# Second pass, layer one: shared sums of block products kept in PSUM, seeded by a ScalarE copy

## The chip, the cores and the metric

One Trainium2 chip, one core. The metric is the device time of one execution of the kernel in microseconds (us). Engines: PE (TensorE matrix products), DVE (VectorE), ACT (ScalarE), POOL (GpSimd) and SP, whose queue issues most transfers. PSUM is the memory that PE writes its sums to, in banks; SBUF is the large on-chip memory.

## The reference

Attention with a sigmoid in place of the softmax feeds a gated network (two weights, a squared relu, a sigmoid gate); its output `x` goes through this last part, in which the change lies:

```python
def _moe2_ref(x, w_ch1, w_ch2) -> np.ndarray:
    X = np.fft.fft(x, axis=1)
    X = np.fft.fft(X, axis=2)
    mixed = np.real(X).astype(np.float32)
    u = x + mixed
    mu = np.mean(u, axis=-1, keepdims=True)
    var = np.mean((u - mu) ** 2, axis=-1, keepdims=True)
    un = (u - mu) / np.sqrt(var + 1e-06)
    ch = np.maximum(un @ w_ch1, 0.0) @ w_ch2
    return (u + ch).astype(np.float32)
```

The batch is 4, the sequence 448, the model width 768; `w_ch1` is 768 x 3072 and `w_ch2` 3072 x 768. All is float32.

## The kernel before, in words

Every large product is made of float32 values split in a high and a low part of 12 bits, with three matmuls (high x high, high x low, low x high) into one PSUM bank of 128 x 448 sums. The last network (`w_ch1` is layer one, `w_ch2` layer two) runs in two passes. The first takes batches 0 and 1 directly. The second pass, which takes batches 2 and 3 together, is where the change lies; it needs fewer products, by Winograd's form of Strassen's scheme: a 2 x 2 block product out of seven block products of sums and differences of the blocks, whose results share partial sums.

Layer one of the second pass is `pair1(g, _)`, called for the twelve groups g = 0 to 11 of 256 hidden columns. Each call takes the seven entries of the table `PRODUCTS` in order; in this document they are n = 0 to 6. An entry names the weight block (A11, S2, ...), the rows block (B11, T2, ...) and the bank (X, Y, Z or W) that its nine matmuls of 448 columns add to. After each product `after(n)` reads its bank:

- n = 0 (A11 B11): ACT copies X to SBUF, `u2`.
- n = 1 (S2 T2): DVE adds bank Y to `u2`.
- n = 2 (S3 T3): DVE makes `u3` = `u2` + Z.
- n = 3 (S1 T1): DVE adds W to `u3`, which is the result block c22 and goes through the relu in `result`.
- n = 4 (A12 B21): added on X by PE; the result is read from the bank.
- n = 5 (A22 T4): added on Z by PE; DVE makes `c21` = `u2` + Z.
- n = 6 (S4 B22): added on W by PE; DVE adds W to `u2`.

PE may add to a bank only when it has been read: `step` starts n = 4 after the ACT copy, n = 5 after `u3`, n = 6 after the c22 add (the `need` of `c1`, `u3`, `c22`).

What else runs at that time. The pass goes `pair1` of groups 0 and 1, and then, five times, `second` (layer two, products k = 0 to 4), `pair1` of an even group, `second` (k = 5 and 6), `pair1` of an odd group. `second_weights` makes the layer-one blocks (`blk`) out of raw weights `a` that SP loads from DRAM, `second_weights2` the layer-two blocks (`sw`) out of raw weights `w` (tiles `w2_1` to `w2_4`, four transfers each), `second_rows` the layer-two rows (`hs`) out of the tile `rows`. All of them cast on ACT and subtract on DVE. `second_done` copies each finished layer-two bank to one of six `stage` slots on ACT and POOL then adds it into DRAM by a transfer (`u_d<-stage`).

The order of the work on each engine is fixed before the launch: the class `Order` keeps a clock with estimated costs (lines 200 to 262 of the profile are its helpers: L200 every matmul, L235 a DVE add or subtract, L252 an ACT copy or cast, L254 an ACT activation, L261 a transfer), and each helper issues its instruction when its inputs should be there by that clock. On the chip each engine takes its instructions in that order, and waits for what an instruction needs even if a later one could run. Banks come from `bank` (two, and a third for every third call) and `bank2` (five).

Of the kernel before, what the change touches and what calls it, by code (L numbers as in the profile page):

```python
# [16 lines left out]
ALU = mybir.AluOpType  # L17
# [3 lines left out]
B, H, S, DH = 4, 12, 448, 64  # L21
# [47 lines left out]
def _dft_tables():  # L69
# [36 lines left out]

PRODUCTS = (
    ("A11", "B11", "X"),
    ("S2", "T2", "Y"),
    ("S3", "T3", "Z"),  # L110
    ("S1", "T1", "W"),
    ("A12", "B21", "X"),
    ("A22", "T4", "Z"),
    ("S4", "B22", "W"),
)
LATE = ("T1", "B21", "T4", "B22")


SECOND = (("A11", "B11"), ("S1", "T1"), ("A12", "B21"), ("S4", "B22"), ("S2", "T2"), ("S3", "T3"), ("A22", "T4"))
# [148 lines left out]
def build(tc, ap):  # L268
    nc = tc.nc
    V, G = nc.vector, nc.gpsimd  # L270
    o = Order(nc)
# [72 lines left out]
    w_d = {nm: [dram.tile([128, D], F32, name=f"{nm}_d{i}") for i in range(2 * NG)] for nm in ("w1", "w2")}  # L344
    t_d = {(nm, d): dram.tile([128, 2, S], F32, name=f"t_d{nm}{d}") for nm in LATE for d in range(3)}
    rs_d = [dram.tile([1, S], F32, name=f"rs_d{b}") for b in range(B)]
# [7 lines left out]
    def bank(name):  # L354
        banked[0] += 1
        if ps1c and banked[0] % 3 == 0:
            return ps1c[0].tile([128, 512], F32, tag="bankc", name=name)
        return ps1.tile([128, 512], F32, tag="bank", name=name)
# [248 lines left out]
    for f in range(NF + KD):  # L607
        if f < NF:
            src, hl, key = ap["w_k"][f], [w[:, f].rearrange(flat) for w in (wkh, wkl)], ("wk", f)
        elif f < NF + HELD:  # L610
            src, hl, key = ap["w_r"][f - NF], [w.rearrange(flat) for w in wr_t[f - NF]], ("wr", f - NF)
# [42 lines left out]
    def bank2(name):  # L654
        return ps1b.tile([128, 512], F32, tag="bank2", name=name)
# [133 lines left out]
    for i, n in enumerate((113, 112, 112, 111)):  # L789
        c = fp.tile([128, 2, TW], F32R, name=f"ct{i}")  # L790
# [335 lines left out]
    def parts_of(out, src, key, eng):  # L1126

        yield o.act(out[0], src)
        o.at[key] = t = o.sub(eng, out[1], src, out[0])
        yield t  # L1130
# [49 lines left out]
    blk_t = {}  # L1180

    def second_weights():

        for g in range(NG):
            w = []
            for j in range(2):
                if g > 0:
                    yield from o.need(("blk", 7 * g - 1))
                t = ws2.tile([128, D], F32, tag=f"w{j}", name=f"a_{g}_{j}", bufs=1)
                at = o.dma(t, w_d["w1"][2 * g + j])  # L1190
                w.append((t, min(at, o.now + 9.0) if g == 1 else at))
            yield max(t for _, t in w)
            (wa, wb), n = (t for t, _ in w), D // 2
            a11, a12, a21, a22 = wa[:, 0:n], wa[:, n:D], wb[:, 0:n], wb[:, n:D]
            s1 = ws2.tile([128, n], F32, tag="s1", name=f"s1_{g}", bufs=1)
            src = {"A11": a11, "S2": a11, "S3": a21, "S1": s1, "A12": a12, "A22": a22, "S4": a12}
            for k, (nm, _, _) in enumerate(PRODUCTS):
                m = 7 * g + k
                if m < 8:
                    yield from o.need(("w1", "used", NG - 2 + m // 4))  # L1200
                else:
                    yield from o.need(("prod", m - 8))
                pl = pools_of["w1"][m % 8 // 4]
                blk_t[m] = pl.tile([128, D], F32R, tag="w1" + "hl"[m % 2], name=f"blk_{m}", bufs=2)
                if nm == "S2":
                    yield o.tt(V, s1, a21, a22, ALU.add)
                    yield o.tt(V, a21, a11, a21, ALU.subtract)
                    yield o.tt(V, a11, s1, a11, ALU.subtract)
                elif nm == "S4":
                    yield o.tt(V, a12, a12, a11, ALU.subtract)  # L1210
                yield from parts_of((blk_t[m][:, 0:n], blk_t[m][:, n:D]), src[nm], ("blk", m), V)
# [42 lines left out]
    def second_rows():  # L1254

        yield from o.need(*(("t_d", nm, 2) for nm in LATE))
        ms = np_.tile([128, 3, 2, S], F32, tag="x2", name="rows", bufs=3)
# [85 lines left out]
    def prepare_rows():  # L1343
# [8 lines left out]
        def put(nm, d, src):  # L1352
            if nm not in LATE:
                t = t_t[nm, d] = tp.tile([128, 2, S], F32R, name=f"{nm}_{d}")
                yield from parts_of((t[:, 0], t[:, 1]), src, ("t", nm, d), V)
                return
            t = np_.tile([128, 2, S], F32R, tag="sq", name=f"{nm}_{d}", bufs=1)
            yield from parts_of((t[:, 0], t[:, 1]), src, ("row", nm, d), V)
            o.at["t_d", nm, d] = t = o.dma(t_d[nm, d], t.bitcast(F32))
            yield t + 2.0  # L1360
# [19 lines left out]
    def late_rows():  # L1380
        for n, (nm, d) in enumerate((nm, d) for nm in LATE for d in range(3)):
            yield from o.need(("w1", "last", n // KD), ("t_d", nm, d))
            t = t_t[nm, d] = kp.tile([128, 2, S], F32R, tag="k2v", name=f"{nm}_{d}", bufs=NK)
            o.at["t", nm, d] = o.dma(t.bitcast(F32), t_d[nm, d])
            yield o.now + 0.2


    def result(g, b, i, src):
        yield from (master if g < 2 * NS else hidden)(g, b, i, src)
# [21 lines left out]
    def network():  # L1411
# [31 lines left out]
        def pair1(g, _):  # L1443

            ps, t = {}, {}

            def tmp(nm):
                tag = {"u2": "sum_u", "u3": "sum_v", "c21": "rsb"}[nm]
                t[nm] = np_.tile([128, S], F32, tag=tag, name=f"{nm}_{g}", bufs=1)
                return t[nm]  # L1450

            def after(n):
                x, y, z, w = (ps[k][:, 0:S] if k in ps else None for k in "XYZW")
                if n == 0:
                    o.at["c1", g] = o.act(tmp("u2"), x)
                elif n == 1:
                    yield from o.need(("c1", g))
                    o.at["u2", g] = o.tt(V, t["u2"], t["u2"], y, ALU.add)
                elif n == 2:
                    yield from o.need(("u2", g))  # L1460
                    o.at["u3", g] = o.tt(V, tmp("u3"), t["u2"], z, ALU.add)
                elif n == 3:
                    yield from o.need(("u3", g))
                    o.at["c22", g] = o.tt(V, t["u3"], t["u3"], w, ALU.add)
                    yield o.at["c22", g]
                    yield from result(g, 3, 1, t["u3"])
                elif n == 4:
                    yield from result(g, 2, 0, x)
                elif n == 5:
                    o.at["c21", g] = o.tt(V, tmp("c21"), t["u2"], z, ALU.add)  # L1470
                    yield o.at["c21", g]
                    yield from result(g, 2, 1, t["c21"])
                else:
                    yield o.tt(V, t["u2"], t["u2"], w, ALU.add)
                    yield from result(g, 3, 0, t["u2"])
                yield o.now

            def step(n, i, lhs, rhs, k):
                if i == 0 and n < 4:
                    ps[k] = (bank2 if k == "Y" else bank)(f"f1_{g}_{k}")  # L1480
                o.mm(ps[k][:, 0:S], lhs, rhs, i == 0 and n < 4, i == 8, skip=True)
                if i == 8:
                    o.at["prod", 7 * g + n] = o.now
                    o.spawn(after(n), o.now + 0.1)

            for n, (_, rows, k) in enumerate(PRODUCTS):
                blk = blk_t.get(7 * g + n)
                yield from o.need(("blk", 7 * g + n))
                yield from o.need(*((key, g) for key in {4: ["c1"], 5: ["u3"], 6: ["c22"]}.get(n, [])))
                blk = blk_t[7 * g + n]  # L1490
                for d in range(3):
                    yield from o.need(("t", rows, d))
                    ws = [blk[:, c : c + 128] for c in (128 * d, D // 2 + 128 * d)]
                    rs = [t_t[rows, d][:, c] for c in range(2)]
                    for i, (a, c) in enumerate(((0, 0), (0, 1), (1, 0))):
                        o.feed.append(partial(step, n, 3 * d + i, ws[a], rs[c], k))
                while len(o.feed) > 6:
                    yield o.now + 0.1
# [39 lines left out]
        for p in range(NS):  # L1538
            order += [(second, "s2", (p, range(5))), (pair1, "p1", (2 * p + 2, 3))]
            order += [(second, "s2", (p, (5, 6))), (pair1, "p1", (2 * p + 3, 3))]  # L1540
# [43 lines left out]
    o.spawn(second_rows())  # L1584
    o.spawn(combine())
    o.spawn(second_weights())
    o.spawn(second_weights2())
    o.run()
# [64 lines left out]
```

## Time and profile before

| | us |
|---|---|
| runs: median of 3 (lowest, highest) | 1159.89 (1159.8, 1160.81) |
| the profiled execution's own time | 1160.56 |
| its span, first to last instruction | 1158.8 |
| PE busy in the span | 1149.8 |
| DVE busy | 792.5 |
| ACT busy | 570.8 |
| layer one and two of the second pass | 848 to 1126 of the span |

The span is one profiled execution; the runs are others, without a profile. In the trace's rows a start is in us from the first instruction. In a timeline row the square bracket is the idle time ahead of the instruction and what ended it. A matmul row lasts longer than it holds the engine, because matmuls overlap; nine matmuls of 448 columns take 1.80 us in the chain of waits, which is what they add to the time. The view of the chain starts a product 0.16 us later than the timeline does.

### The profile page before, as it was taken

How to read it: one execution, taken by the hardware profiler on the slowest of the kernel's cores; microseconds unless marked ns; L12 is line 12 of the kernel's file. 1: busy time of each engine (PE TensorE's matmuls, PEld its weight loads, DVE VectorE, ACT ScalarE, POOL GpSimd, SP SyncE). 2: the span in 40 equal slices, each digit the busy share in tenths (PEclk: the TensorE clock that was granted, in tenths of full speed). 3: DMA queues.
4: the chain of work that ended last, by engine and by line, in shares of the span. 5: the costliest groups of instructions: out<-in, count | busy, mean ns of one | idle time of the engine just before them, and what ended most of it. 6: DMA issues, size and time to landing. Idle time of an engine off the chain costs nothing.

```text
span 1158.8 us, 16593 instructions
## 1 busy us (share of the span) xinstructions
PE 1149.8 (99%) x6094; PEld 1009.0 (87%) x6094; DVE 792.5 (68%) x1333; ACT 570.8 (49%) x1051; POOL 106.7 (9%) x154
## 2 busy tenths in 40 slices
PE   8999999999999999999999999999999999999998
PEld 3476676799999999999999999999999999999998
DVE  3876757576514679898777767775477787777662
ACT  6887887667520133243333333332137567665740
POOL 0000001000000000000000000000003243342420
PEclk9999999999999999999999999999999999999999
DMA  7765789668939355477575657563917696878894
GB/s 234 238 230 201 255 325 336 237 230 285 335 136 290 121 191 199 138 287 273 201 252 195 227 190 236 186 228 123 339 44 176 128 201 109 186 137 170 177 195 167
DMA packets 92550, 243.53 MB, mean 210 GB/s; under 512 B 10610, under 2 KB 46516, under 8 KB 92340
## 3 DMA queue, kind: packets, MB, share of 16 engines
q1 hardware_dynamic: 74596, 204.70, 50.8%
q0 software_dynamic: 17584, 37.30, 17.1%
q8 instruction: 48, 0.79, 0.3%
q10 hardware_dynamic: 288, 0.46, 0.1%
q14 instruction: 34, 0.28, 0.1%
HBM read 145.45 MB, written 99.04 MB: 211 GB/s over the span
## 4 chain that ended last, share of the span: by engine, by line
PE 96%; DMA 1%; ACT 1%; DVE 0%; issue 0%; SPq 0%; DVEq 0%
PE f L200 32%; PE m L200 10%; PE v L200 10%; PE k L200 9%; PE r L200 7%; PE av L200 6%; PE sc L200 5%; PE f_W L200 4%; PE f_X L200 3%; PE f_Z L200 3%; PE f_Y L200 2%; PE pq L200 1%; DMA w<-w_d 1%; PE sc_c L200 1%; PE pa L200 1%; PE qa L200 1%
## 5 line engine op out<-in xcount | busy, mean ns | idle before, releaser
L200 PE MATMUL f<-un,w1h 128*128 128x448 f32 x576 | 164.2, 364 | 0.0
L200 PE MATMUL f<-h,w2h 128*128 128x448 f32 x576 | 163.2, 363 | 0.0
L235 DVE TENSOR_TENSOR acc<-acc,f 128x448 f32<-128x448 f32 x126 | 77.6, 619 | 70.9 <-PE f L200 69.4
L259 POOL DMA_DIRECT2D u_d<-stage x75 | 64.7, 933 | 604.1 <-ACT stage L252 597.1
L200 PEld LDWEIGHTS f<-un,w1h 128*128 128x128 f32 x576 | 108.1, 188 | 7.6 <-issue 0.6
L200 PEld LDWEIGHTS f<-h,w2h 128*128 128x128 f32 x576 | 108.1, 188 | 7.1
L200 PE MATMUL v<-k,wvh 128*128 128x448 f32 x384 | 111.9, 365 | 0.0
L200 PE MATMUL f<-un,w1l 128*128 128x448 f32 x288 | 103.9, 361 | 0.0
L200 PE MATMUL f<-h,w2l 128*128 128x448 f32 x288 | 103.7, 360 | 0.0
L200 PE MATMUL m<-hs,sw_h 128*128 128x448 f32 x324 | 91.5, 363 | 0.0
L254 ACT ACTIVATE sg<-sc,bias_s 128x448 f32<-128x448 f32 x144 | 78.6, 651 | 13.2 <-PE sc L200 13.2
L200 PEld LDWEIGHTS v<-k,wvh 128*128 128x128 f32 x384 | 72.0, 188 | 4.9 <-issue 0.6
L200 PE MATMUL k<-xkh,wkh 128*128 128x448 f32 x192 | 70.6, 368 | 0.9 <-ACT kt L254 0.9
L200 PE MATMUL k<-xkl,wkh 128*128 128x448 f32 x192 | 70.2, 366 | 0.0
L200 PE MATMUL k<-xkh,wkl 128*128 128x448 f32 x192 | 70.1, 365 | 0.0
L200 PE MATMUL v<-k,wvl 128*128 128x448 f32 x192 | 69.7, 363 | 0.0
L254 ACT ACTIVATE h<-f 128x448 fp32r<-128x448 f32 x48 | 26.2, 546 | 81.1 <-PE f L200 81.1
L200 PEld LDWEIGHTS m<-hs,sw_h 128*128 128x128 f32 x324 | 60.8, 188 | 4.0
L252 ACT COPY stage<-m 128x448 f32<-128x448 f32 x105 | 55.7, 535 | 16.0 <-DMA u_d<-stage 9.4
L200 PE MATMUL m<-hs,sw_l 128*128 128x448 f32 x162 | 58.3, 360 | 0.0
L200 PEld LDWEIGHTS f<-un,w1l 128*128 128x128 f32 x288 | 53.9, 187 | 3.9 <-issue 0.2
L200 PE MATMUL av<-sg,v 128*64 128x448 f32 x288 | 57.2, 544 | 0.0
(227 smaller groups left out, 2490.2 us busy)
## 6 DMA issues: line engine op xcount, KB each, us to landing
w_raw<-in_w SPq DMA_DIRECT2D x40, 768.0 KB, 4.9
u_d<-stage POOLq DMA_DIRECT2D x75, 224.0 KB, 6.1
w_d<-w_bits SPq DMA_DIRECT2D x40, 384.0 KB, 2.6
k_d<-kp SPq DMA_DIRECT2D x32, 448.0 KB, 3.9
k<-k_d SPq DMA_DIRECT2D x32, 448.0 KB, 5.6
a<-w_d SPq DMA_DIRECT2D x24, 384.0 KB, 5.5
w<-w_d SPq DMA_DIRECT2D x24, 384.0 KB, 10.4
v<-in_v SPq DMA_DIRECT2D x24, 256.0 KB, 3.5
```

The costliest lines, as they stand in the source:

```text
L200: self.nc.tensor.matmul(out, lhs, rhs, start=start, stop=stop, skip_group_check=skip)
L235: eng.tensor_tensor(out, a, c, op=op)
L252: self.nc.scalar.copy(out, a)
L254: self.nc.scalar.activation(out, a, fn, **kw)
L259: self.nc.gpsimd.dma_start(out, src, accum_op=ALU.add)
```

## The change

The three partial sums are no longer made on DVE but in PSUM, by PE's own addition. The order of the products changes and Z is gone:

- n = 0 (A11 B11) in X; ACT copies bank X into bank Y (the seed).
- n = 1 (S3 T3) in W; ACT copies W to SBUF, `w7`.
- n = 2 (S2 T2) is added on the seed in Y; ACT copies Y to SBUF, `u2`.
- n = 3 (A12 B21) is added on X; the result is read from the bank.
- n = 4 (S1 T1) is added on Y; DVE adds Y to `w7`, which is c22.
- n = 5 (A22 T4) is added on W; DVE adds W to `u2`, which is c21.
- n = 6 (S4 B22) is added on Y; the result is read from the bank.

PE now starts n = 2 after the seed, n = 4 after the copy `u2`, n = 5 after the copy `w7`, n = 6 after the c22 add. X and W come from `bank2`, Y from `bank`. The rows blocks that are loaded late are loaded in the new order of use (B21 ahead of T1).

```diff
@@ -106,14 +106,14 @@
 
 PRODUCTS = (
     ("A11", "B11", "X"),
+    ("S3", "T3", "W"),
     ("S2", "T2", "Y"),
-    ("S3", "T3", "Z"),
-    ("S1", "T1", "W"),
     ("A12", "B21", "X"),
-    ("A22", "T4", "Z"),
-    ("S4", "B22", "W"),
+    ("S1", "T1", "Y"),
+    ("A22", "T4", "W"),
+    ("S4", "B22", "Y"),
 )
-LATE = ("T1", "B21", "T4", "B22")
+LATE = ("B21", "T1", "T4", "B22")
 
 
 SECOND = (("A11", "B11"), ("S1", "T1"), ("A12", "B21"), ("S4", "B22"), ("S2", "T2"), ("S3", "T3"), ("A22", "T4"))
@@ -1202,7 +1202,7 @@
                     yield from o.need(("prod", m - 8))
                 pl = pools_of["w1"][m % 8 // 4]
                 blk_t[m] = pl.tile([128, D], F32R, tag="w1" + "hl"[m % 2], name=f"blk_{m}", bufs=2)
-                if nm == "S2":
+                if nm == "S3":
                     yield o.tt(V, s1, a21, a22, ALU.add)
                     yield o.tt(V, a21, a11, a21, ALU.subtract)
                     yield o.tt(V, a11, s1, a11, ALU.subtract)
@@ -1445,48 +1445,43 @@
             ps, t = {}, {}
 
             def tmp(nm):
-                tag = {"u2": "sum_u", "u3": "sum_v", "c21": "rsb"}[nm]
+                tag = {"u2": "sum_u", "w7": "sum_v", "c": "rsb"}[nm]
                 t[nm] = np_.tile([128, S], F32, tag=tag, name=f"{nm}_{g}", bufs=1)
                 return t[nm]
 
             def after(n):
-                x, y, z, w = (ps[k][:, 0:S] if k in ps else None for k in "XYZW")
+                x, y, w = (ps[k][:, 0:S] if k in ps else None for k in "XYW")
                 if n == 0:
-                    o.at["c1", g] = o.act(tmp("u2"), x)
+                    ps["Y"] = bank(f"f1_{g}_Y")
+                    o.at["seed", g] = o.act(ps["Y"][:, 0:S], x)
                 elif n == 1:
-                    yield from o.need(("c1", g))
-                    o.at["u2", g] = o.tt(V, t["u2"], t["u2"], y, ALU.add)
+                    o.at["w7", g] = o.act(tmp("w7"), w)
                 elif n == 2:
-                    yield from o.need(("u2", g))
-                    o.at["u3", g] = o.tt(V, tmp("u3"), t["u2"], z, ALU.add)
+                    o.at["u2", g] = o.act(tmp("u2"), y)
                 elif n == 3:
-                    yield from o.need(("u3", g))
-                    o.at["c22", g] = o.tt(V, t["u3"], t["u3"], w, ALU.add)
+                    yield from result(g, 2, 0, x)
+                elif n == 4:
+                    o.at["c22", g] = o.tt(V, t["w7"], t["w7"], y, ALU.add)
                     yield o.at["c22", g]
-                    yield from result(g, 3, 1, t["u3"])
-                elif n == 4:
-                    yield from result(g, 2, 0, x)
+                    yield from result(g, 3, 1, t["w7"])
                 elif n == 5:
-                    o.at["c21", g] = o.tt(V, tmp("c21"), t["u2"], z, ALU.add)
-                    yield o.at["c21", g]
-                    yield from result(g, 2, 1, t["c21"])
+                    yield o.tt(V, t["u2"], t["u2"], w, ALU.add)
+                    yield from result(g, 2, 1, t["u2"])
                 else:
-                    yield o.tt(V, t["u2"], t["u2"], w, ALU.add)
-                    yield from result(g, 3, 0, t["u2"])
+                    yield from result(g, 3, 0, y)
                 yield o.now
 
             def step(n, i, lhs, rhs, k):
-                if i == 0 and n < 4:
-                    ps[k] = (bank2 if k == "Y" else bank)(f"f1_{g}_{k}")
-                o.mm(ps[k][:, 0:S], lhs, rhs, i == 0 and n < 4, i == 8, skip=True)
+                if i == 0 and n < 2:
+                    ps[k] = bank2(f"f1_{g}_{k}")
+                o.mm(ps[k][:, 0:S], lhs, rhs, i == 0 and n < 2, i == 8, skip=True)
                 if i == 8:
                     o.at["prod", 7 * g + n] = o.now
                     o.spawn(after(n), o.now + 0.1)
 
             for n, (_, rows, k) in enumerate(PRODUCTS):
-                blk = blk_t.get(7 * g + n)
                 yield from o.need(("blk", 7 * g + n))
-                yield from o.need(*((key, g) for key in {4: ["c1"], 5: ["u3"], 6: ["c22"]}.get(n, [])))
+                yield from o.need(*((key, g) for key in {2: ["seed"], 3: ["seed"], 4: ["u2"], 5: ["w7"], 6: ["c22"]}.get(n, [])))
                 blk = blk_t[7 * g + n]
                 for d in range(3):
                     yield from o.need(("t", rows, d))
```

Where the instructions stand. The first place is DVE in group 6, around the add that n = 6 of PE waits for. Names: `sw_3` is the sum of raw layer-two weights made from `w2_3`; `u3_6` + `f1_6_W` is c22 before. Before:

```order
L235 TENSOR_TENSOR sw_21_l_9814<-w2_3_9729,sw_21_h_9813 128x768
L235 TENSOR_TENSOR u3_6_9825<-u2_6_9791,f1_6_Z_9804 128x448
L235 TENSOR_TENSOR blk_48_9808<-a_6_0_9567,blk_48_9808 128x384
L235 TENSOR_TENSOR sw_3_9812<-w2_3_9729 128x768
L235 TENSOR_TENSOR u3_6_9825<-u3_6_9825,f1_6_W_9823 128x448
L235 TENSOR_TENSOR w2_3_9729<-w2_3_9729 128x2x384
L235 TENSOR_TENSOR w2_3_9729<-sw_3_9812,w2_3_9729 128x2x384
L235 TENSOR_TENSOR c21_6_9865<-u2_6_9791,f1_6_Z_9804 128x448
```

And now, where `w7_6` + `f1_6_Y` is c22:

```order
L235 TENSOR_TENSOR blk_48_9776<-a_6_0_9541,blk_48_9776 128x384
L235 TENSOR_TENSOR sw_21_l_9802<-w2_3_9713,sw_21_h_9801 128x768
L235 TENSOR_TENSOR sw_3_9800<-w2_3_9713 128x768
L235 TENSOR_TENSOR w2_3_9713<-w2_3_9713 128x2x384
L235 TENSOR_TENSOR w2_3_9713<-sw_3_9800,w2_3_9713 128x2x384
L235 TENSOR_TENSOR w7_6_9791<-w7_6_9791,f1_6_Y_9778 128x448
L235 TENSOR_TENSOR u2_6_9811<-u2_6_9811,f1_6_W_9774 128x448
```

The c22 add stood behind one instruction on the raw weights `w2_3`, and stands behind three now; in group 8 it is the same.

The second place is DVE in group 2, before (c22 is the second row with `u3_2`):

```order
L235 TENSOR_TENSOR u3_2_8865<-u2_2_8837,f1_2_Z_8852 128x448
L235 TENSOR_TENSOR sw_7_l_8871<-w2_1_8780,sw_7_h_8870 128x768
L235 TENSOR_TENSOR u3_2_8865<-u3_2_8865,f1_2_W_8863 128x448
L235 TENSOR_TENSOR sw_1_8869<-w2_1_8780 128x768
L235 TENSOR_TENSOR w2_1_8780<-w2_1_8780 128x2x384
L235 TENSOR_TENSOR w2_1_8780<-sw_1_8869,w2_1_8780 128x2x384
L235 TENSOR_TENSOR c21_2_8905<-u2_2_8837,f1_2_Z_8852 128x448
```

And now (c22 is `w7_2`):

```order
L235 TENSOR_TENSOR sw_7_l_8847<-w2_1_8764,sw_7_h_8846 128x768
L235 TENSOR_TENSOR sw_1_8845<-w2_1_8764 128x768
L235 TENSOR_TENSOR w2_1_8764<-w2_1_8764 128x2x384
L235 TENSOR_TENSOR w2_1_8764<-sw_1_8845,w2_1_8764 128x2x384
L235 TENSOR_TENSOR w7_2_8851<-w7_2_8851,f1_2_Y_8832 128x448
```

Here the c22 add stood ahead of the three, and stands behind them now. In group 4 it stood behind the first of them and now stands behind the first two.

The third place is ACT in group 10, at the copy of bank X. Now (before, the same rows stand ahead of the copy `u2_10<-f1_10_X`, though in a slightly other order):

```order
L252 CAST hs_34_1_10696<-rows_8109 128x448
L252 COPY stage_8315<-m_32_1_10681 128x448
L252 CAST blk_75_10705<-a_10_1_10490 128x384
L252 COPY stage_8315<-m_32_2_10693 128x448
L252 COPY f1_10_Y_10728<-f1_10_X_10709 128x448
L252 CAST blk_76_10726<-a_10_0_10488 128x384
L252 COPY w7_10_10741<-f1_10_W_10724 128x448
L252 CAST v2_0_0_h_10750<-w2_5_10663 128x768
L252 COPY u2_10_10760<-f1_10_Y_10728 128x448
```

The copy of X has kept its place behind the same two `stage` copies; it is now the seed of n = 2, and two more copies follow it.

## Rows read from the trace of the kernel before

**Rows 1.** The page, busy time, share of the span and instructions by engine:

```profile
PE 1149.8 (99%) x6094; PEld 1009.0 (87%) x6094; DVE 792.5 (68%) x1333; ACT 570.8 (49%) x1051; POOL 106.7 (9%) x154
```

**Rows 2.** Windows: length, busy PE, PEld, DVE, ACT, POOL, granted clock, DMA share, GB/s:

```profile
0.00:8.00 8.00, 4.07 (x12) 1.86 (x12) 0.12 (x2) 3.32 (x6) 0.33 (x6) 1.00 0.72 221
...
848.00:1126.00 278.00, 277.77 (x1389) 259.99 (x1388) 209.53 (x336) 175.12 (x348) 90.37 (x105) 1.00 0.76 153
```

**Rows 3.** Waits of PE: who waited for whom, us in total, times, longest:

```profile
PE sc L200 <- DMA q<-in_q: 3.9, 1, 3.9
...
PE f_W L200 <- DVE u L235: 0.2, 1, 0.2
```

**Rows 4.** Chain that ended last, second pass: start, us, what:

```profile
891.57 1.80 PE f_X L200 x9
...
911.37 1.80 PE f_X L200 x9
...
923.98 18.00 PE m L200 x90
941.98 1.80 PE f_X L200 x9
...
961.79 1.80 PE f_X L200 x9
...
986.49 0.88 DVE sw_l L235
...
988.80 12.90 DMA w<-w_d
...
1002.67 0.62 DVE u L235
...
1003.43 2.05 PE f_W L200 x9
...
1012.70 1.80 PE f_X L200 x9
...
1043.30 1.80 PE f_X L200 x9
...
1093.71 1.80 PE f_X L200 x9
```

**Rows 5.** Timeline of DVE in group 2: start, us, instruction, idle before:

```profile
898.81 0.62 DVE L235 TENSOR_TENSOR u<-u,f_W 128x448 f32<-128x448 f32 x1
901.32 0.96 DVE L235 TENSOR_TENSOR sw<-w 128x768 f32<-128x768 f32 x1 [1.89 <-DMA w<-w_d]
902.31 0.96 DVE L235 TENSOR_TENSOR w<-w 128x768 f32<-128x768 f32 x1
903.30 0.96 DVE L235 TENSOR_TENSOR w<-sw,w 128x768 f32<-128x768 f32 x1
904.18 0.61 DVE L235 TENSOR_TENSOR c<-u,f_Z 128x448 f32<-128x448 f32 x1
```

**Rows 6.** Timeline of DVE in groups 4, 6 and 8, the same instruction:

```profile
950.71 0.96 DVE L235 TENSOR_TENSOR sw<-w 128x768 f32<-128x768 f32 x1 [1.15 <-DMA w<-w_d]
...
1001.80 0.96 DVE L235 TENSOR_TENSOR sw<-w 128x768 f32<-128x768 f32 x1 [1.86 <-DMA w<-w_d]
...
1051.61 0.96 DVE L235 TENSOR_TENSOR sw<-w 128x768 f32<-128x768 f32 x1 [1.35 <-DMA w<-w_d]
```

**Rows 7.** The tile f_X: ACT's copies, count, shortest/median/longest ns:

```profile
L252 ACT COPY u<-f_X x12: 531/535/540, 850.2 to 1115.4; 128x448 f32<-128x448 f32 x12
```

**Rows 8.** Timeline of ACT, copies of bank X in groups 2, 3, 10:

```profile
894.87 0.54 ACT L252 COPY u<-f_X 128x448 f32<-128x448 f32 x1
...
913.75 0.53 ACT L252 COPY u<-f_X 128x448 f32<-128x448 f32 x1
...
1096.48 0.53 ACT L252 COPY stage<-m 128x448 f32<-128x448 f32 x1 [1.93 <-DMA u_d<-stage]
1096.91 0.54 ACT L252 COPY u<-f_X 128x448 f32<-128x448 f32 x1
```

## The prediction

> **What bounds the kernel now.** I read the page first, then the windows, the waits of PE, the chain, and last the timelines of DVE and ACT beside the changed order. PE is busy for 1149.8 of 1158.8 us [rows 1]. In the stretch of the change, 848 to 1126 us, it is busy for 277.77 of 278.00 us at a granted clock of 1.00 [rows 2]: the change can win there only what PE waits. That is one wait, 0.2 us on DVE's `u` [rows 3]. The chain shows where it comes from: DVE ends a layer-two cast (`sw_l`), four transfers of raw weights `w` follow and take 12.90 us, DVE has an instruction that waits for them, and behind it stands the add `u` at 1002.67, after which PE's last product of group 6 starts at 1003.43 [rows 4]. The reader is to see that DVE, busy for 209.53 of the 278 us [rows 2], has time to spare, and yet one of its adds is late, because of what stands ahead of it.
>
> **What one late add costs.** Seven products take 12.60 us, and layer two's 90 matmuls 18.00. Group 5 starts at 961.79, so group 6 starts at 992.39 and its product n = 6 is due 6 x 1.80 later, at 1003.19. The add ended at 1003.29, only 0.10 late. But group 7 starts at 1012.70, where 992.39 + 12.60 + 36 x 0.20 would be 1012.19 [rows 4]. The 0.10 cost 0.51: each stop costs its lateness and 0.41 more (signal, refilling). I take lateness + 0.41 for every new stop.
>
> **Part 1, the work removed and added.** Each of the 12 groups loses three DVE adds and gains two ACT copies, while one ACT copy changes its target. At 0.61 us an add [rows 5] DVE is rid of 36 x 0.61 = 22 us; at 0.535 us a copy [rows 7] ACT gains 24 x 0.535 = 12.8 us. PE waits for neither as long as they are in time, so both are worth 0; the cover is 1.80 us of the other product between producer and user. If that cover is gone the price is the lateness + 0.41. A copy from PSUM to PSUM occurs nowhere before. Its nearest row is the copy from PSUM to SBUF, 531 to 540 ns, which I take; the ends are 0 and twice that, which adds some 0.5 us in the one place where a copy is late (below), and little elsewhere.
>
> **Part 2, the seed.** PE used to need the copy of X after three more products; now after one, 3.60 us after the group's start. In group 3 the copy ends at 913.75 + 0.53 = 914.28 against 911.37 + 3.60 = 914.97: in time. In group 2 it ends at 895.41 against 895.17, late by 0.24, and in group 10 at 1097.45 against 1097.31, late by 0.14, because ACT stands at a `stage` copy until a transfer frees its slot [rows 4, 8]. In group 10 that costs 0.14 + 0.41 = **0.55 us**. In group 2 the later stop (below) is counted from the same DVE instruction, and the seed's delay is part of it. The other groups resemble group 3.
>
> **Part 3, c22, the main term.** PE's n = 6 needs c22. Before, c22 was made after n = 3, with two products of cover; now it comes after n = 4, with one, and in the even groups the order puts it behind DVE's instructions on the raw weights: `sw`, which waits for the transfers, and then two more in groups 2, 6 and 8, one more in group 4. In group 2 the instructions start at 901.32, 902.31 and 903.30, and the next add runs from 904.18 to 904.79 [rows 5]. So c22 ends 3.47 us after the start of `sw`, or 2.48 with one instruction fewer (0.99). The transfers are issued by SP after DVE's last `sw_l`, which the change leaves where it was to within one short instruction, so I keep the starts of `sw` [rows 5, 6]. Against due times of group start + 10.80 [rows 4]:
>
> - group 2: 904.79 - 902.37 = 2.42, + 0.41 = **2.83**
> - group 4: 950.71 + 2.48 = 953.19 - 952.78 = 0.41, + 0.41 = **0.82**
> - group 6: 1001.80 + 3.47 = 1005.27 - 1003.19 = 2.08, + 0.41 = 2.49, less the 0.51 that it loses already: **1.98**
> - group 8: 1051.61 + 3.47 = 1055.08 - 1054.10 = 0.98, + 0.41 = **1.39**
> - group 10 has no such instructions: 0. The odd groups: 0.
>
> Queued behind the waiting `sw` on DVE are c22, c21 and the casts' subtractions; those who wait are PE (c22) and ACT, whose relu of c22 has room.
>
> **Part 4, the rest.** The banks' new pools and the late rows' order move no product ahead of what it needs, and PE waits for neither a bank nor late rows in this stretch before [rows 3]; worth 0. If that failed it would cost a stop of about 0.41 per group.
>
> **Sum.** 2.83 + 0.82 + 1.98 + 1.39 + 0.55 = 7.57 us on the profiled execution's 1160.56 (span 1158.8 and 1.76 around it), 1168.1. The median of the runs shown is 1159.89, 0.67 less: I forecast **1167.5 us**.
>
> **The range.** The open size is when the transfers land. `sw` starts 9.75, 8.73, 9.41 and 8.31 us after its group's start. If all landed as the earliest does, the stops would be 1.39, 0.40, 1.39 and 1.39; less 0.51, plus 0.55, that is 4.6, or 1164.5. If all landed as the latest, 2.83, 1.82, 2.83, 2.83, less 0.51, plus 0.55: 10.4, or 1170.2. `sw_l`, ahead of them, may move by about an instruction of 0.5 us, 0.5 for each of the four; half of that below gives 1163.5, most of it above 1172.0. The forecast's own range is 1163.5 to 1172.0.
>
> **Rivals.**
>
> *The transfers come early (not slower).* DVE is rid of 22 us, and the transfers hang on a DVE instruction. If `w` were in SBUF before c22 is ready, no stop would be left: c22 would be late nowhere, the 0.51 of group 6 would go and the 0.55 of group 10 stay, 1159.9 us. It decides at `sw` starting 10.80 - 3.47 = 7.3 us after a group's start, against 8.31 to 9.75 now, so the transfers must be 1 to 2.4 us earlier in all groups. For it: their start hangs on DVE. Against it: DVE's time is freed in `pair1`, while `sw_l` runs during `second`, 6 us before group 6 [rows 4], where no add is removed. Chance 0.10. It is within 0.2% of before, about what a measurement of this kernel can tell from no change. Clearly faster has no mechanism: PE waits 0.23 us in the stretch.
>
> *The transfers land later.* The loads of `a` now start sooner, since the last block's subtraction has fewer adds ahead of it, and may share the way with `w`. Four transfers take 12.90 us [rows 4], some 3.2 each; half of one lost to sharing is 1.6 us in groups 4, 6 and 8, + 4.8: 1172.3. No row shows it. Chance 0.10. By the Trainium skill, DMA: Bandwidth & Descriptors, section Queues, rings and completion order, each engine consumes the descriptors of one queue in ring order; by that rule loads of the same queue issued later would hold up nothing, and the sum would stay at 1167.5; no row here tests it.
>
> *PE's clock falls.* After stops of 2 to 3 us the clock may fall to its lower level of 1.2 GHz. If one product of 1.80 us [rows 4] after each of the four c22 stops took twice its time, that is 4 x 1.80 = 7.2 us: 1174.7. Against it: the windows show 1.00 throughout, also in the first 8 us [rows 2], in which PE waits 3.9 us at the start [rows 3]; PE has no stop between busy stretches as long as the new ones, though, so it isn't excluded. Chance 0.04. The Trainium skill, TensorE: Matmul & The Clock Gate, section HAM oscillation, states that idle gaps of PE bring the lower clock back; by it the longer stops are where to look, while the start of this trace does not show it.
>
> *The bank doesn't keep the seed.* If PE's first matmul on Y overwrote what ACT wrote, the sums would lack X, but PE's instructions and waits would be the same: 1167.5. It has no chance of its own in the time.
>
> **How the numbers follow.** Forecast 0.74, early transfers 0.10, late transfers 0.10, clock 0.04; 0.02 for faster by means that I don't see. The predicted time is the forecast's, 1167.5. The range 1163.5 to 1172.0 is the forecast's own and leaves out the early case, the clock, the unseen and about half of the late case, just under 2 in 10, 0.2 with what the forecast itself may miss. Slower by over 0.2% (2.3 us) hold the forecast, the late case and the clock, 0.88; within 0.2% the early case, 0.10; faster 0.02.
>
> **What would show it.** Right: PE's waits name DVE's `w` add ahead of f_Y in groups 2, 4, 6 and 8, the longest in group 2 at 2 to 3 us and the shortest in group 4; DVE idle at `sw` for the transfers, and the c22 add directly behind the instructions on `w`; a wait for ACT's copy into f_Y of some 0.1 to 0.3 us in groups 2 and 10 alone. Wrong: no such waits, or stops in the odd groups too (then ACT's copies are the cause), or a wait of PE for `stage` copies (then the banks are), or `sw` starting at another distance from its group, or a granted clock below 1.00 behind a stop.

## The result and the profile after

The changed kernel took **1168.64 us** (median of 4 runs, 1166.82 to 1170.16) beside 1159.85 us (1159.80 to 1160.81) for the kernel before in the same comparison: a ratio of 1.0071 [1.0058, 1.0084], slower by 8.8 us. The forecast was 1167.5 us, the range 1163.5 to 1172.0. The execution that was profiled is the slowest of the four, 1170.16 us (span 1168.4), against 1160.56 (span 1158.8) before: 9.6 us more, and those are what the rows below account for.

The page, busy time by engine, which answers to [rows 1]:

```profile
PE 1153.2 (99%) x6094; PEld 1011.4 (87%) x6094; DVE 775.8 (66%) x1297; ACT 582.4 (50%) x1075; POOL 106.5 (9%) x154
```

DVE lost 16.7 us of work and ACT gained 11.6 us. Neither shows in the time. The waits of PE (who waited for whom, us in total, times, longest), which answer to [rows 3]:

```profile
PE f_Y L200 <- DVE w L235: 5.3, 2, 2.7
PE sc L200 <- DMA q<-in_q: 4.0, 1, 4.0
...
PE f_Y L200 <- ACT f_Y L252: 0.9, 1, 0.9
```

Two new kinds of wait, on the add that makes c22 (DVE `w`) and on the seed (ACT `f_Y`): 6.2 us of PE standing still, where the kernel is 9.6 us slower. The rest is found behind the stops. PE's timeline (start, us, instruction, count, idle before): the late product of group 2, then of group 6 the fifth and sixth product, the late seventh and layer two behind it, then the late one of group 8:

```profile
895.18 2.07 PE L200 MATMUL f_Y<-T,blk 128*128 128x448 f32 x9 [0.89 <-ACT f_Y L252]
...
1000.09 1.96 PE L200 MATMUL f_Y<-T,blk 128*128 128x448 f32 x9
1001.89 1.96 PE L200 MATMUL f_W<-T,blk 128*128 128x448 f32 x9
1006.57 2.96 PE L200 MATMUL f_Y<-B,blk 128*128 128x448 f32 x9 [2.71 <-DVE w L235]
1009.33 0.95 PE L200 MATMUL m<-extra,sw_h 128*128 128x448 f32 x2
...
1061.45 3.21 PE L200 MATMUL f_Y<-B,blk 128*128 128x448 f32 x9 [2.61 <-DVE w L235]
```

Nine matmuls of one product take 1.96 us; behind the two long stops they take 2.96 and 3.21, behind the short one 2.07. The windows (us, busy PE, PEld, DVE, ACT, POOL, granted clock, DMA share, GB/s) say why:

```profile
1003.00:1006.00 3.00, 0.85 (x5) 0.46 (x3) 2.90 (x4) 0.83 (x1) 0.00 (x0) 1.00 0.88 214
1006.50:1008.00 1.50, 1.43 (x6) 1.33 (x7) 1.50 (x4) 1.40 (x3) 0.00 (x0) 0.83 0.03 6
1008.00:1010.00 2.00, 2.00 (x7) 1.79 (x6) 1.40 (x3) 0.50 (x2) 0.00 (x0) 0.50 0.00 0
1010.00:1012.00 2.00, 2.00 (x9) 1.81 (x9) 1.40 (x3) 1.56 (x4) 0.00 (x0) 0.78 0.00 0
1012.00:1014.00 2.00, 2.00 (x12) 1.88 (x11) 1.68 (x3) 1.28 (x3) 1.37 (x2) 1.00 0.28 14
...
1063.00:1065.00 2.00, 2.00 (x7) 1.80 (x6) 1.29 (x3) 0.31 (x1) 0.00 (x0) 0.50 0.00 0
```

After the stop PE is busy without a gap, but at a granted clock that goes down to 0.50, the 1.2 GHz level: 7 matmuls in 2.00 us where 12 stand later. The three rows from 1006.50 to 1012.00 lose 0.17 x 1.50 + 0.50 x 2.00 + 0.22 x 2.00 = 1.70 us to the clock, and group 6 loses 1.7 us beyond the late start of its product. The last row shows the same behind the stop of group 8. [Rows 2] had 1.00 throughout.

Why the add is late shows on DVE: group 2, where it is in time, and group 6, where it isn't (start, us, instruction, idle before):

```profile
898.35 0.96 DVE L235 TENSOR_TENSOR sw<-w 128x768 f32<-128x768 f32 x1 [1.48 <-DMA w<-w_d]
...
901.21 0.61 DVE L235 TENSOR_TENSOR w<-w,f_Y 128x448 f32<-128x448 f32 x1
...
1003.03 0.96 DVE L235 TENSOR_TENSOR sw<-w 128x768 f32<-128x768 f32 x1 [3.73 <-DMA w<-w_d]
1004.03 0.96 DVE L235 TENSOR_TENSOR w<-w 128x768 f32<-128x768 f32 x1
1005.02 0.96 DVE L235 TENSOR_TENSOR w<-sw,w 128x768 f32<-128x768 f32 x1
1005.89 0.61 DVE L235 TENSOR_TENSOR w<-w,f_Y 128x448 f32<-128x448 f32 x1
```

The chain is the one that was forecast: an idle DVE, three instructions on the raw weights, and the add directly behind them. In group 6 it ends at 1006.50, 2.81 us after PE's due time of 992.89 + 10.80 = 1003.69 (group starts in this part are the timeline's; by the chain's, which the forecast used, it is 0.16 less, 2.65). And why the seed is late, ACT in group 2:

```profile
891.60 0.53 ACT L252 COPY stage<-m 128x448 f32<-128x448 f32 x1 [2.40 <-DMA u_d<-stage]
...
893.75 0.53 ACT L252 COPY stage<-m 128x448 f32<-128x448 f32 x1 [0.68 <-DMA u_d<-stage]
894.17 0.51 ACT L252 CAST blk<-a 128x384 fp32r<-128x384 f32 x1
894.59 0.54 ACT L252 COPY f_Y<-f_X 128x448 f32<-128x448 f32 x1
```

Where the time went, group by group: a group's loss is the next group's start less its own, less 12.60 and layer two's time between them (7.20 us behind an even group, 18.00 behind an odd one). The odd groups lose 0.01 us or less in each of these kernels, so only the even ones stand here; the last four lines are experiments.

| us lost in group | 2 | 4 | 6 | 8 | 10 | sum |
|---|---|---|---|---|---|---|
| forecast | 2.83 | 0.82 | 2.49 | 1.39 | 0.55 | 8.08 |
| changed kernel | 1.17 | 0.38 | 4.57 | 4.51 | 0.39 | 11.02 |
| c22 add first | 1.31 | 0.53 | 0.84 | 1.49 | 0.01 | 4.18 |
| seed first | 1.25 | 2.56 | 4.55 | 4.22 | 0.01 | 12.59 |
| both first | 0.01 | 0.25 | 0.02 | 0.14 | 0.01 | 0.43 |
| loads of `a` later | 0.64 | 0.16 | 2.41 | 3.67 | 0.00 | 6.88 |

The kernel before lost 0.51 (group 6), so the changed one lost 10.5 us more in the stretch; its first group starts 0.89 us sooner (847.31 for 848.20), which leaves the 9.6.

### The profile page after: what moved, and what is told of

Same layout as the page of the kernel before. It is cut to its first block, busy times and chain, and to the rows that moved or that the text cites. A ratio compares the mean times of both kernels' runs of the same rounds, so it can differ in the third digit from the quotient of the medians.

```text
span 1168.4 us, 16548 instructions
## 1 busy us (share of the span) xinstructions
PE 1153.2 (99%) x6094; PEld 1011.4 (87%) x6094; DVE 775.8 (66%) x1297; ACT 582.4 (50%) x1075; POOL 106.5 (9%) x154
## 4 chain that ended last, share of the span: by engine, by line
PE 48%; issue 41%; POOL 5%; DMA 3%; ACT 2%; DVE 1%; POOLq 0%; ACTq 0%; DVEq 0%
PE v L200 10%; PE k L200 9%; PE r L200 7%; PE av L200 6%; PE sc L200 4%; POOL u_d L259 4%; PE f L200 4%; DMA u_d<-stage 2%; POOL m_d L259 1%; PE f_Y L200 1%; PE pq L200 1%; PE sc_c L200 1%; PE m L200 1%; PE pa L200 1%; PE qa L200 1%
## 5 line engine op out<-in xcount | busy, mean ns | idle before, releaser
L252 ACT COPY stage<-m 128x448 f32<-128x448 f32 x105 | 55.1, 534 | 22.4 <-DMA u_d<-stage 13.4
L235 DVE TENSOR_TENSOR blk<-a,blk 128x384 fp32r<-128x384 f32 x72 | 39.8, 555 | 27.1 <-ACT blk L252 26.6
```

The costliest lines, as they stand in the source:

```text
L235: eng.tensor_tensor(out, a, c, op=op)
L252: self.nc.scalar.copy(out, a)
```

## The experiments

**1. The c22 add ahead of the instructions on `w`.** In the function that makes layer two's weights:

```diff
                 if nm == "S1":
+                    if p > 0:
+                        yield from o.issued(("c22", 2 * p))
                     yield o.tt(V, s1, a21, a22, ALU.add)
```

> One edit to the changed kernel: in groups 2, 4, 6 and 8 VectorE's c22 add stands ahead of the three instructions that work on the raw w (behind it until now). Queue theory (TensorE stops because the add waits in VectorE's order behind instructions that wait for the w transfers): the stops of groups 6 and 8 go, with the half clock behind them (4.57 and 4.51 us in the profiled run), only the late seeds stay (1.94 us in all): about 1161 us, and no wait of f_Y on DVE w of over 0.3 us. Rival, the add is late of itself (it waits for its product or for ScalarE's w copy): the same stops at the same places, 1168.6 us. Rival, the stop moves on to what now stands behind the three instructions (the u add that frees W, the blk parts of the next group): 1162 to 1166 us, with f_W or a blk tile as the tile that TensorE waits for.

Measured: 1163.02 us (11 runs), ratio 1.0019 [1.0011, 1.0028]. PE's waits:

```profile
PE f_Y L200 <- ACT f_Y L252: 2.2, 2, 1.2
...
PE m L200 <- ACT stage L252: 0.4, 1, 0.4
```

and DVE in group 6 (start, us, instruction, idle before):

```profile
1002.92 0.62 DVE L235 TENSOR_TENSOR w<-w,f_Y 128x448 f32<-128x448 f32 x1 [2.43 <-PE f_Y L200]
1003.46 0.95 DVE L235 TENSOR_TENSOR sw<-w 128x768 f32<-128x768 f32 x1
```

No wait on c22 is left. The add now waits for its own product, and `sw` behind it waits for nothing: in the same place the order alone had made PE stop. About two thirds of the slowdown (8.8 us down to 2.8, each beside its own runs of the kernel before) go with an edit that only orders instructions. The clock is 1.00 over the profiled run. The time is 2 us above what was expected: seeds late in groups 2 and 8 (1.31 and 1.49 us), late copies by ACT and one wait of 0.4 us for a `stage` copy cost 4.2 us here and not 1.9.

**2. The seed ahead of the last `stage` copies.**

```diff
         def second_done(p, k, e, ps):
+        if k == 4 and e > 0:
+            yield from o.issued(("seed", 2 * p + 2))
         st = m_t["stage"][:, (3 * (7 * p + k) + e) % KD]
```

> One edit to the changed kernel: ScalarE's last two stage copies of product k=4 stand behind the seed copy of the even group, ahead of it until now. Theory (the seed is late because stage copies ahead of it wait for a slot): no PE wait of f_Y on ACT f_Y, the 1.17, 0.38 and 0.39 us of groups 2, 4 and 10 go, and the stops behind c22 stay: about 1166.7 us. Rival, the w part of the delay grows by what the seed gives back, because the w transfers land at the same absolute time: 1168 us or more, with the c22 stops longer by as much. Rival, bank release: the first product X or W waits for a bank whose stage copy now comes later, a new wait on f_X or f_W, over 1169 us.

Measured: 1169.90 us (6 runs, 1165.81 to 1172.59), ratio 1.0080 [1.0062, 1.0097]: no gain over the change as it is. The seed's waits are gone, and PE stops at c22 in all four groups instead (PE's timeline, groups 2, 4, 6, 8):

```profile
903.33 2.08 PE L200 MATMUL f_Y<-B,blk 128*128 128x448 f32 x9 [0.96 <-DVE w L235]
...
956.30 2.08 PE L200 MATMUL f_Y<-B,blk 128*128 128x448 f32 x9 [2.28 <-DVE w L235]
...
1009.66 3.52 PE L200 MATMUL f_Y<-B,blk 128*128 128x448 f32 x9 [2.67 <-DVE w L235]
...
1064.29 3.53 PE L200 MATMUL f_Y<-B,blk 128*128 128x448 f32 x9 [2.35 <-DVE w L235]
```

The time is the first rival's. A stop for the seed gives the transfers time to land, so the two causes can hide behind each other: in group 2 of the changed kernel the add was in time only because the seed had held the group up by 1.17 us. Group 4 is not explained by that alone: its stop of 2.28 us is far longer than the 0.38 us that the seed gives back, because `sw` starts 9.71 us after the group's start, for 8.16 in the changed kernel. Why `w` lands later there stays open.

**3. Both edits.**

> Both edits at once. Theory: every stop that the change made is gone, and so is the 0.5 us that the kernel before lost in group 6: 1159.0 to 1160.0 us, the same as before or under it by up to 0.5 us, with the granted clock at 1.00 through the groups. Rival, ACT copies into PSUM slow TensorE's own writes into the other banks: groups take more than 12.60 us each without any wait, 1161 us or more.

Measured: 1160.40 us (12 runs, 1159.98 to 1162.09), ratio 1.0002 [0.9994, 1.0011]: the kernel before, to within what can be told, and 0.4 us above the expected range. PE's waits:

```profile
PE sc L200 <- DMA q<-in_q: 3.8, 1, 3.8
PE k L200 <- ACT kt L254: 0.9, 3, 0.5
```

None lies in the stretch of the change. So the sums in PSUM, the seeds written by ACT and the new banks cost PE next to nothing in themselves (0.43 us in the stretch, where the kernel before lost 0.51); the slowdown is order. Nor do they win anything: DVE has less to do, and PE didn't wait for DVE.

**4. The loads of `a` later.** A copy of two columns by ACT, which can run only after the group's fourth product, holds them back:

```diff
+                if g in (5, 7, 9):
+                    yield from o.need(("m", g - 1, 2, 0))
                 t = ws2.tile([128, D], F32, tag=f"w{j}", name=f"a_{g}_{j}", bufs=1)
+                if g in (5, 7, 9):
+                    o.act(t[:, 0:2], m_t[(g - 1) % 2, 2][:, 0, 0:2])
```

> One edit to the changed kernel, on transfers alone: the loads of a for groups 5, 7 and 9 start only after the fourth product of groups 4, 6 and 8 has been evacuated (a two-column ScalarE copy into a stands ahead of them), about 7.9 us after the group's start as in the kernel before, in place of 3.9 to 4.3 us. Theory A (a's load shares the transfer engines with w and makes it land later): sw starts in groups 6 and 8 at 8.3 to 9.4 us after the group's start as before, in place of 10.1, the two stops shrink by 0.7 and 1.7 us, and with them some or all of the half clock: 1163.5 to 1166.5 us. Theory B (w's landing has nothing to do with a, but with the accumulating stage transfers or chance): sw still starts 10 us after, 1168.6 us.

Measured: 1165.06 us (5 runs), ratio 1.0038 [1.0025, 1.0051], clear of the change's own interval. DVE in groups 6 and 8:

```profile
1001.58 0.96 DVE L235 TENSOR_TENSOR sw<-w 128x768 f32<-128x768 f32 x1 [2.04 <-DMA w<-w_d]
...
1054.07 0.96 DVE L235 TENSOR_TENSOR sw<-w 128x768 f32<-128x768 f32 x1 [2.65 <-DMA w<-w_d]
```

`sw` starts 9.56 and 9.24 us after its group (992.02 and 1044.83), for 10.14 and 10.05 with the change and 9.57 and 8.47 before (timeline starts of 992.23 and 1043.14; the prediction's 9.41 and 8.31 go by the chain's). From SP's issue of the loads of `w` it is 14.23 and 13.91 us, for 14.80 and 14.71. Theory A, then, as far as one trace of each kernel shows it: loads of `a` that start sooner make `w` land 0.6 and 0.8 us later. In group 6 that is all of the delay, in group 8 half of it. The time fell by more than that, because no half clock follows the stop of group 6 here (PE's timeline, groups 6 and 8):

```profile
1005.11 2.08 PE L200 MATMUL f_Y<-B,blk 128*128 128x448 f32 x9 [1.81 <-DVE w L235]
...
1057.60 2.65 PE L200 MATMUL f_Y<-B,blk 128*128 128x448 f32 x9 [1.80 <-DVE w L235]
```

The two stops are of the same length, and only the second is followed by the half clock, so their length alone doesn't decide that.

**5. Stops of five lengths.** The kernel with both edits, and ahead of c22 in five odd groups some adds more:

```diff
+                    for _ in range({1: 3, 3: 4, 5: 5, 7: 6, 9: 7}.get(g, 0)):
+                        o.tt(V, t["c"] if "c" in t else tmp("c"), t["w7"], y, ALU.add)
                     o.at["c22", g] = o.tt(V, t["w7"], t["w7"], y, ALU.add)
```

> The kernel with both edits, plus 3, 4, 5, 6 and 7 more VectorE adds that read bank Y ahead of the c22 add in groups 1, 3, 5, 7 and 9 (they write a scratch tile): stops of TensorE of about 0.6, 1.1, 1.7, 2.2 and 2.7 us, made at 0.54 us an add. Theory (a longer stop is followed by a stretch at the half clock, a shorter one is not): the nine matmuls after the stop take 1.96 to 2.1 us in groups 1, 3 and 5 and about 3 us in group 9, group 7 is open; the time is the 1160.4 us of both edits + 8.3 us of stops + 0.2 us a stop for the restart + 1.0 to 1.5 us for each stop with the half clock: 1170.5 to 1173 us. Rival (the half clock had to do with something else in groups 6 and 8, such as the transfers, and follows no stop here): 1.00 throughout, 1169.7 us or less.

Measured: 1176.61 us (4 runs), 16.2 over both edits. PE's timeline, groups 1, 3, 5, 7 and 9:

```profile
871.63 2.08 PE L200 MATMUL f_Y<-B,blk 128*128 128x448 f32 x9 [0.88 <-DVE w L235]
...
923.95 2.06 PE L200 MATMUL f_Y<-B,blk 128*128 128x448 f32 x9 [1.62 <-DVE w L235]
...
976.89 2.06 PE L200 MATMUL f_Y<-B,blk 128*128 128x448 f32 x9 [2.27 <-DVE w L235]
...
1030.50 3.37 PE L200 MATMUL f_Y<-B,blk 128*128 128x448 f32 x9 [2.93 <-DVE w L235]
...
1086.32 3.70 PE L200 MATMUL f_Y<-B,blk 128*128 128x448 f32 x9 [3.58 <-DVE w L235]
```

An add more lengthens the stop by 0.65 us, not by 0.54, so the stops and the time came out above the expectation. The kind of result is the theory's, and its rival falls: three stops cost their lateness and 0.10 to 0.12 us more, the two longest cost 1.66 and 2.86 us on top, at the half clock. Group 7, say: the product starts at 1030.50, 3.10 us after 1016.60 + 10.80, and group 8 starts 4.76 us late.

**6. Five equal stops.** The same with 6 adds in each of the five groups.

> The same with 6 adds in each of groups 1, 3, 5, 7 and 9: five equal stops of about 2.2 us. If the length of the stop decides alone, the nine matmuls behind it take the same time in all five groups, all about 2.1 us or all about 3 us; if something else has a say (when the stop falls), some are followed by the half clock and others not. Time: 1160.4 + 5 x (2.2 + 0.2) = 1172.4 us with no half clock, up to 1180 us with it behind all five.

Measured: 1183.88 us (4 runs), 23.5 over both edits; again the stops are longer than meant, 2.84 to 2.94 us. The half clock followed all five, at a cost over the lateness of 1.71, 1.70, 1.68, 1.55 and 2.91 us. The windows behind the first and the last stop:

```profile
874.00:876.00 2.00, 1.96 (x9) 1.79 (x10) 1.97 (x4) 1.11 (x2) 0.00 (x0) 0.88 0.00 0
876.00:878.00 2.00, 2.00 (x7) 1.78 (x6) 1.00 (x3) 1.43 (x3) 0.00 (x0) 0.50 0.00 0
878.00:880.00 2.00, 2.00 (x10) 1.81 (x9) 0.97 (x3) 0.98 (x3) 0.00 (x0) 0.77 0.00 0
...
1094.70:1097.00 2.30, 2.30 (x6) 2.08 (x7) 0.85 (x2) 1.04 (x2) 0.00 (x0) 0.50 0.43 106
1097.00:1099.00 2.00, 2.00 (x7) 1.74 (x7) 0.00 (x0) 0.57 (x2) 0.00 (x0) 0.50 0.73 278
1099.00:1101.00 2.00, 2.00 (x7) 1.78 (x6) 1.16 (x2) 1.22 (x3) 0.00 (x0) 0.55 0.00 2
```

At this size every stop was followed by it, at two prices: the fall comes 1 to 2 us into the work after the first stop and is there from the start after the last, where it also lasts longer. The rows lose 0.12 x 2.00 + 0.50 x 2.00 + 0.23 x 2.00 = 1.70 us to the clock behind the first stop and 0.50 x 2.30 + 0.50 x 2.00 + 0.45 x 2.00 = 3.05 behind the last, close to the 1.71 and 2.91 that the groups lost: the price is the time that PE works at the half clock, halved. What sets the moment and the length stays open.

**7. The kernel before, with its add moved behind.** No seed, no sums in PSUM; only the order of DVE in groups 2, 4, 6 and 8 (`three` is noted when the three instructions on `w` are issued):

```diff
                 elif n == 3:
                     yield from o.need(("u3", g))
+                    if g in (2, 4, 6, 8):
+                        yield from o.issued(("three", g))
                     o.at["c22", g] = o.tt(V, t["u3"], t["u3"], w, ALU.add)
```

> The kernel before, with its four banks and its VectorE sums, and one edit: in groups 2, 4, 6 and 8 its c22 add stands behind the three VectorE instructions on the raw w (ahead of them until now). Queue theory: the order alone makes the slowdown, without a seed and without sums in PSUM: the add ends 3.5 us after sw starts (at 9.75, 8.73, 9.41 and 8.31 us after the group's start), TensorE wants it at 10.8 us, so stops of 2.4, 1.4, 2.1 and 1.0 us, with restart and half clock 1167 to 1171 us. Rival (the slowdown belongs to what else the change does, ScalarE's copies, the accumulation in one bank): no stop of over 0.5 us, 1160 to 1161.5 us.

Measured: 1172.75 us (6 runs, 1168.83 to 1175.89), ratio 1.0107 [1.0090, 1.0124]. DVE in group 4:

```profile
952.45 0.96 DVE L235 TENSOR_TENSOR sw<-w 128x768 f32<-128x768 f32 x1 [1.90 <-DMA w<-w_d]
953.44 0.96 DVE L235 TENSOR_TENSOR w<-w 128x768 f32<-128x768 f32 x1
954.43 0.96 DVE L235 TENSOR_TENSOR w<-sw,w 128x768 f32<-128x768 f32 x1
955.31 0.61 DVE L235 TENSOR_TENSOR u<-u,f_W 128x448 f32<-128x448 f32 x1
```

PE stands 1.52, 2.18, 1.47 and 1.53 us in the four groups of the profiled run, which took 1168.83, and the groups lose 1.80, 4.02, 1.74 and 1.80 us, the second with the half clock. The order alone makes as large a slowdown as the whole change, in a kernel that has none of the rest. The median lies 1.75 us above the expected range. The other five runs took longer than the profiled one and have a lower mean granted clock (0.994 to 0.997, the profiled one 0.998): more of their stops were followed by the half clock, it seems, but no row here shows it.

## Why the prediction was right, point by point

**The bound and the mechanism: right, and shown.** PE had nothing to win, and lost where a DVE add stands behind instructions that wait for `w`. Runs 1 and 7 show it from both sides: moving the add ahead takes some 6 us off the change, moving it behind puts 12 us on the kernel before.

**Part 1, work removed and added worth 0: right** (run 3). DVE gave up 16.7 us, not 22. The copy from PSUM to PSUM, taken at 535 ns from [rows 7], took 526 in the median (517 to 542).

**Part 2, the seed: mis-sized.** The step that failed is the seed's lateness of 0.24 us in group 2 and 0.14 in group 10, read off the copies' times before: it kept the `stage` copies where they were. ACT's waits for a `stage` slot grew from 9.4 to 13.4 us, and seeds were late in groups 2, 4 and 10: 1.17 + 0.38 + 0.39 = 1.94 us instead of 0.55; with the c22 stops gone, most of 4.2 us (run 1).

**Part 3, c22: right in kind, wrong by group.** The step that failed is "I keep the starts of `sw`" [rows 5, 6]. Measured from the group's start, by the timeline before and after, they moved by -2.09, -0.73, +0.57 and +1.58 us in groups 2, 4, 6 and 8. In 2 and 4 `w` landed sooner, and the late seed held PE up by 1.17 and 0.38 us, so the add was in time. In 6 and 8 `w` landed later, 0.6 and 0.8 us of it through the loads of `a` (run 4); the other half in group 8 stays open. By the chain's due times the lateness came to 0 + 0 + 2.65 + 2.56 = 5.2 us, where 5.89 was forecast (2.42 + 0.41 + 2.08 + 0.98).

**Lateness + 0.41: right for a short stop, too little for a long one.** The forecast counts the lateness of the add against the chain's due time. Counted so, stops without the half clock cost 0.33 to 0.41 us on top: in group 3 of run 5 the add ends at 923.80, 1.48 us after 911.36 + 0.16 + 10.80, and the group loses 1.89. (The 0.10 to 0.12 us of run 5 is the same rest counted from the late start of the product.) The two long stops of the changed kernel cost 4.57 - 2.65 = 1.92 and 4.51 - 2.56 = 1.95 on top. The 0.41 came from one short stop, which could not show the clock.

**The rivals: the one held unlikely came, two came in part.** The clock had 0.04. "PE has no stop between busy stretches as long as the new ones" was the reason not to exclude it, and should have weighed more: it fell after both long stops, some 1.7 us each beyond the product's late start. That is the rule of the Trainium skill, TensorE: Matmul & The Clock Gate, section HAM oscillation, which the prediction named: idle gaps bring the lower clock back; the trace agrees (0.50 behind stops of 2.71 and 2.61 us), and shows it behind shorter gaps than those in that section's example.

The reason against the clock was misread. The windows give 1.00 for the first 8 us [rows 2], but in the chain before, the first twelve `sc` matmuls, behind the wait of 3.9 us at the start, take twice as long as the next twelve:

```profile
3.93 4.85 PE sc L200 x12
...
10.15 2.46 PE sc L200 x12
```

That is what the half clock would give, though no row names it as the cause; the start spoke for the rival and not against it.

The rival of transfers that land later was true in two of its three groups at half its price (0.6 and 0.8 us, not 1.6). The rival of early transfers came in part in the other two even groups (2.09 and 0.73 us sooner). The Trainium skill, DMA: Bandwidth & Descriptors, section Queues, rings and completion order, states in what order descriptors are consumed; that later loads of the same queue would then hold up nothing was my conclusion from it. Run 4 differs (`w` lands 0.6 to 0.8 us sooner without them), and the measurement decides, though it doesn't show by which way they share.

**The total was nearer than its parts, by luck.** From the 8.08 us of the forecast's groups go the two stops that didn't come (3.65); on top come 1.39 for the seeds, 2.15 for the later add in groups 6 and 8 and 3.05 for what the two long stops cost over 0.41. Of the 11.02 us that makes, 4.3 stood in the forecast at their place (2.49, 1.39 and 0.39 in groups 6, 8 and 10). The missing stops and the dearer ones nearly cancelled, which nothing in the prediction saw; two of its own signs of being wrong showed (`sw` at another distance from its group, a granted clock below 1.00 behind a stop). Forecast, late transfers and clock were priced as cases that exclude one another; all three happened in one run.

Two slips in the arithmetic change nothing: in the range the 1.82 of group 4 should be 1.84, and the chances that the range leaves out add up to 0.21, not to just under 0.2.

## What to carry to other kernels

When a change moves an instruction later on an engine that works in order, look at what it now stands behind: an add of 0.6 us, on an engine that is idle a third of the time, cost some 6 us here because its neighbours wait for a transfer, and two lines that order it gave that back. Taking work off an engine that nobody waits for won nothing here. Two late producers on one path can hide each other: mending the seed alone won nothing, mending both won all. Price a stop of TensorE in two sizes: a short one by its lateness, one of some 2 us or more, as seen here, by that and a possible stretch at the half clock.

## What was not expected of the hardware

The granted clock falls to 0.50 already after stops of some 2 us between long busy stretches. Over all profiled runs, none of the stops of 0.33 to 1.62 us inside the stretch of the change was followed by it, and every one of 2.35 to 3.58 us was. Between them both are seen: 1.81, 2.27 and 2.28 us without, 1.80 and 2.18 us with. Beyond the late start it cost 1.5 to 1.7 us a time in most cases and 2.9 in two. The kernel before has no such stop in this stretch, and its trace could show neither figure.
